# Hash attention with a squared-ReLU MLP: sign bits by eight small transfers in GpSimd's queue, weight exponents in four single steps, x in four pieces, the last pair's sums in another order

## Chip, cores and metric

The kernel runs on one core of a Trainium2 chip. The metric is device time in microseconds (us) of one execution; lower is better. The time before is a median of three runs. A profile of one execution shows every instruction of the engines TensorE (PE, with its weight loads as PEld), VectorE (DVE), ScalarE (ACT), GpSimd (POOL) and of SyncE (SP), which only issues transfers here.

## The reference, cut to what matters

```python
# q, k, v: (4, 8, 768, 64) float32; proj: (64, 6) float32
q_bits = (einsum('bhsd,dk->bhsk', q, proj) > 0)          # six sign bits of each query
k_bits = (einsum('bhsd,dk->bhsk', k, proj) > 0)          # and of each key
mask   = bucket(q_bits)[:, :, :, None] == bucket(k_bits)[:, :, None, :]
scores = where(mask, q @ k.T / 8, -1e9)
attn   = softmax(scores)                                 # sum + 1e-9 below the line
x      = (attn @ v) rearranged to (3072, 512)
out    = (max(x @ w_in, 0) ** 2) @ w_out                 # w_in (512, 2048), w_out (2048, 512)
```

`w_in` and `w_out` arrive as 64-bit floats, and the kernel makes 32-bit floats of them itself, from the two 32-bit halves of each number.

## The kernel before

**Two parts.** The first 334 us are the attention; the rest is the MLP, written as nested sums and differences of blocks (a Strassen-like scheme) and not touched by the change, apart from where its first inputs are prepared. Engine instructions run in the order in which the program issues them (`tc.manual_schedule()`), each engine in its own queue; waits between engines are put in by dependency.

**The attention loop** goes over 16 pairs of heads (`for pr in range(NP)`, pairs 0 to 15). Six key blocks of 128 keys (`kt`) and two halves of 384 queries (`i`) make twelve steps of `score` in a pair. A `score` multiplies first the bits (`st<-bits`, L431) and then the features (`st<-feat`, L431) into a PSUM buffer `st`; the bits add a large negative number wherever the buckets differ. ACT then writes `e`, the exponential (`weight`, L437). Two buffers of the ring `turn` serve `st` and the hash products; `e` has a ring of four. `attend` (L487) multiplies `e` with the values, in order written out by hand between the scores, and `add_up` (L469, L474, on DVE) sums `e` over key blocks into `total`. `sum_up` (L536) sums `total` over partitions into `tot`, `invert` (L549 to L559) and `spread` (L570) make reciprocals of it, and `normalize` (L579, L585) scales the pair's result and stores it in the DRAM buffer `x_all`. `sum_up`, `invert`, `spread` and `normalize` of a pair run inside the next pair.

**GpSimd's queue.** `attend` and `sum_up` change row halves of PE now and then; at each such point `part` (L482) puts a `memset` of a single element, `token`, in POOL's queue. It waits for the last matmul before the change, and the first one behind it waits for the token. There are four in a pair: at `attend(pr, 0, 1)`, `attend(pr, 2, 0)`, the old pair's `attend(old, 4, 1)`, and in `sum_up`. POOL does nothing else in the loop, except that at pair 12 (`X_0`) it issues the load of the MLP's first chunk of x, `load_x(0)` (L639), 2 MB in a single transfer.

**The bits of the next pair.** Early in a pair PE makes the products with `proj` (`hash_bits`, L365) for the next pair. ACT takes the sign (L384) and multiplies by per-partition gains (L387) into the SBUF tile `signed`, whose partitions are four groups (queries or keys, first or second half) of 32. ACT's own queue stores `signed` in DRAM (`bits_d`, L388). In `place_bits` (L395), behind `score(pr, 4, 0)`, ACT's queue loads it back with two transfers that put the rows where the score needs them, in `all_bits`, double-buffered over pairs.

**The weights.** In each pair one piece of a weight (128 x 1024 numbers) is turned: `part_power` (L151, DVE) cuts the exponent out, `place_power` on ACT converts it in two halves (`g`) of two operations each (L164 to `small`, L165 back to `power`), `part_top` (L173, L177, DVE) and `round_weight` (L191, L194, DVE) finish it. `sum_in` (L601, DVE) forms sums of the pieces of `w_in`, one or two in some pairs. SP issues the loads of the pieces, the loads of q, k (`load_pair`, L305) and v (L314), the stores of `x_all` (L590) and of the weights' sums (L219).

**The end of the attention.** Behind the loop DVE makes four differences of x (`sum_x(0, n)`, L601, tiles `t_x`) for the first MLP product, among the last pair's `add_up`, `invert` and `normalize`. PE begins the MLP (`acc`, L824) right after the last `spread`.

Of the kernel before, what the change touches and what calls it, by code (L numbers as in the profile page):

```python
# [8 lines left out]
FP32 = mybir.dt.float32  # L9
BF16 = mybir.dt.bfloat16  # L10
# [3 lines left out]
U8 = mybir.dt.uint8  # L14
ACTF = mybir.ActivationFunctionType
# [19 lines left out]
def kernel(  # L35
# [10 lines left out]
    nc = tc.nc  # L46
    PSUM = bass.MemoryType.PSUM

    B, H, S, D = q.shape
    NBITS = proj.shape[1]  # L50
    DM = H * D
    DFF = moe_w_in.shape[1]
    P = 128
    SB = S // P
    HS = S // 2
    NFT = DM // P
    NFF = DFF // P
    NP = B * H // 2
    PB = H // 2
# [49 lines left out]
    def spare(name):  # L109

        return ps_t.tile([P, 2, 512], FP32, name=name, tag="spare")
# [42 lines left out]
        )  # L154
        parts[i] = power

    def place_power(i, g):


        if i not in parts:  # L160
            return
        power = parts[i][:, g]
        small = p_w.tile([P, PIECE], U8, name="small", bufs=1)
        nc.scalar.activation(out=small, in_=power, func=ACTF.Relu, bias=excess)  # L164
        nc.scalar.activation(out=power, in_=small, func=ACTF.Copy, scale=2.0**23)  # L165

    def part_top(i):

# [14 lines left out]
    def round_weight(i):  # L183

        raw = raws.pop(i, None)
        if raw is None:
            return keep_weight(i)
        goals[i] = goal(i)
        power, top = parts.pop(i)
        one = top.bitcast(FP32)  # L190
        nc.vector.scalar_tensor_tensor(  # L191
            out=one, in0=raw[:, :, :, 0], scalar=2.0**-32, in1=top, op0=ALU.mult, op1=ALU.add,
        )
        nc.vector.scalar_tensor_tensor(  # L194
            out=goals[i], in0=one, scalar=2.0**-20, in1=power.bitcast(FP32),
            op0=ALU.mult, op1=ALU.mult,
        )
        keep_weight(i)
# [43 lines left out]
    ring = [const.tile([P, 2, 2, HS + 1], FP32, name=f"e{i}") for i in range(NRING)]  # L242
    signed = const.tile([P, 2, HS], BF16, name="signed")
    all_bits = [const.tile([P, 2, S], BF16, name=f"bits{i}") for i in range(2)]
    bits_d = p_d.tile([P, 2, HS], BF16, name="bits_d")

    def constants():
        N = NBITS
# [132 lines left out]
    def signs(pr):  # L381


        nc.scalar.activation(  # L384
            out=signed, in_=hashed[pr, 0][:, :, 0:HS], func=ACTF.Sign, scale=HUGE, bias=lifts
        )
        nc.scalar.activation(out=signed, in_=signed, func=ACTF.Copy, scale=gains)  # L387
        nc.scalar.dma_start(out=bits_d, in_=signed)  # L388

    def place_bits(pr):  # L390

        t = all_bits[pr % 2]
        src = bits_d.rearrange("(g r) h c -> h r g c", r=NR_B)
        for h in range(2):
            nc.scalar.dma_start(  # L395
                out=t[h * D:h * D + NBITS + 1].rearrange("r w (c n) -> r (w c) n", c=2),
                in_=src[h, 0:NBITS + 1],
            )
        for w in range(2):
            bits[pr, w] = t[:, w]  # L400

    def first_keys(c, banks):

# [37 lines left out]
    def score(pr, kt, i, st=None):  # L441

        own = [feat[pr][:, w] for w in range(2)]
        marks = [bits[pr, w] for w in range(2)]
        st = st or turn("st")
        products(st, i, kt, marks, True)
        products(st, i, kt, own, False)
        weight(pr, kt, i, st)
# [44 lines left out]
    def attend(pr, kt, s):  # L493


        if (kt, s) == (0, 0):
            outs[pr] = ps_o.tile([P, 2, 512], FP32, name="xo")
        for r in range(2):
            for h in range(2):
                done = value(  # L500
                    pr, kt, slice(r * HK, (r + 1) * HK), h, (r + s) % 2,
                    (kt, s) == (0, 0), (kt, s) == (SB - 1, 1),
                )
                if turned.get(pr, s) != s:
                    part(lasts[pr], done)
                turned[pr] = s
        lasts[pr] = done
# [58 lines left out]
    def spread(pr):  # L566

        both = onces.pop(pr)
        for h in range(2):
            nc.tensor.matmul(  # L570
                out=spares[pr][h * D:(h + 1) * D, 0, HS:HS + 2 * NB], lhsT=picks,
                rhs=both[:, h].rearrange("p c n -> p (c n)"), start=True, stop=True,
            )
# [59 lines left out]

    xs = {}

    def load_x(i):

        x = p_c.tile([P, NFT, NCH], FP32, name="x")
        nc.gpsimd.dma_start(out=x, in_=x_all[:, :, i * NCH:(i + 1) * NCH])  # L639
        xs[i] = x, [p_c.tile([P, 2, NCH // 2], FP32, name=f"t_x{n}") for n in range(3)]  # L640

    w_unit = {}

# [5 lines left out]
    def load_unit(n, pool=p_i):  # L649

        if n < NCHUNK * NR and n not in w_unit:
            r = order(n)
            w_unit[n] = pool.tile([P, 7, NFT // 2, P], FP32, name="w_unit", bufs=2 if pool is p_i else 1)
            m = 7 if n < NR else 5
            nc.sync.dma_start(out=w_unit[n][:, 0:m], in_=w_in_7[r, :, 0:m])

    def sum_x(i, n):

        x, (t1, t2, t3) = xs[i]
        lo, hi = slice(0, NCH // 2), slice(NCH // 2, NCH)  # L660
        b11, b12, b21, b22 = x[:, 0:2, lo], x[:, 0:2, hi], x[:, 2:4, lo], x[:, 2:4, hi]
        minus(*((t1, b12, b11), (t2, b22, t1), (t3, b22, b12), (b12, b21, t2))[n - 1])

    with tc.manual_schedule():
# [21 lines left out]
        for pr in range(NP):  # L686
            more, old = pr + 1 < NP, pr - 1

            def beside(kt, s):
                if pr > 0:  # L690
                    attend(old, kt, s)

            if pr + 2 < NP:
                load_pair(pr + 2)
            if pr == X_0:
                load_x(0)
            if more and pr > 0:
                features(pr + 1)
            if pr == 0:
                first_score()  # L700
                first_keys(1, spare("hash"))
            else:
                score(pr, 0, 0)
                attend(old, 4, 0)
                score(pr, 0, 1)
                attend(old, 5, 0)
                add_up(old, SB - 1)
                if pr == 1:
                    part_top(0)
                round_weight(old)  # L710
                if more:
                    load_weight(pr + 1)
                for m in sums.get(pr, ()):
                    sum_in(m)
            score(pr, 1, 0)
            beside(4, 1)
            score(pr, 1, 1)
            beside(5, 1)
            if pr == 0:
                features(1)  # L720
            else:
                keep_x(old)
                sum_up(old, 0)
                if more:
                    hash_bits(pr + 1, turn("hash"))
                    signs(pr + 1)
                else:
                    score(pr, 2, 0)
                sum_up(old, 1)
                invert(old)  # L730
            add_up(pr, 1)


            if pr == X_0 + 1:
                for n in range(2):
                    load_unit(n)
            part_power(pr)
            if pr == 0:
                attend(pr, 0, 0)
            if more:  # L740
                score(pr, 2, 0)
            if pr > 0:
                attend(pr, 0, 0)
            else:
                attend(pr, 1, 0)
            score(pr, 2, 1)
            if pr > 0:
                attend(pr, 1, 0)
                place_power(pr, 0)
            else:  # L750
                hash_bits(1, turn("hash"))
                signs(1)
            score(pr, 3, 0)
            if pr > 0:
                spread(old)
            attend(pr, 0, 1)
            score(pr, 3, 1)
            attend(pr, 1, 1)
            add_up(pr, 2)
            if pr > 0:  # L760
                normalize(old)
                place_power(pr, 1)
            add_up(pr, 3)
            if more:
                load_values(pr + 1)


            score(pr, 4, 0)
            if more:
                place_bits(pr + 1)  # L770
            attend(pr, 2, 1)
            score(pr, 4, 1)
            attend(pr, 3, 1)
            if pr > 0:
                part_top(pr)
            score(pr, 5, 0)
            if more:
                attend(pr, 2, 0)
            score(pr, 5, 1, spare("st") if not more else None)
            attend(pr, 3, 0)  # L780
            if pr == 0:
                for g in range(2):
                    place_power(0, g)
            add_up(pr, 4)
        pr = NP - 1
        attend(pr, 2, 0)
        attend_whole(pr, SB - 2)
        sum_x(0, 1)
        add_up(pr, SB - 1)
        for s in range(2):  # L790
            sum_up(pr, s, True)
        invert(pr)
        for n in (2, 3):
            sum_x(0, n)
        attend_whole(pr, SB - 1)
        keep_x(pr)
        spread(pr)
        normalize(pr)
        sum_x(0, 4)
        round_weight(pr)  # L800
        first.close()

# [793 lines left out]
```

## Time and profile before

| | |
|---|---|
| time, median of 3 runs | 882.53 us (880.44, 882.53, 882.84) |
| the profiled execution | 881.52 us, its span 879.7 us |
| mean granted TensorE clock | 0.995 |
| PE, DVE, ACT, POOL busy | 859.9, 751.6, 353.0, 123.8 us |
| first matmul of the MLP | 334.2 us after the span's start |

The span is the time from the first to the last instruction. Busy time of matmuls is modelled, since they are pipelined: a PE that is busy all the time may still be waiting a little between two matmuls. In a timeline row the brackets give the idle time of the engine before the row and what ended it; `ACTq` and `SPq` are the issues of transfers. In group rows the numbers behind the bar are busy us and mean ns of one instruction, then idle us before them. In the chain of waits a row that begins with DMA is a transfer that something waited for.

### The profile page before, as it was taken

What the parts mean: (1) busy time and instruction counts of PE and PEld (TensorE: products, weight loads), DVE (VectorE), ACT (ScalarE), POOL (GpSimd) and SP (SyncE); (2) the same over time, 40 slices, a digit from 0 to 9 for tenths busy, and PEclk for the clock granted to TensorE, in tenths of its full rate; (3) what the DMA queues carried; (4) which work ended last, traced back from release to release, by engine and by line L of the source; (5) the groups of instructions that cost most, each with busy time, mean ns of one, the idle gap of its engine ahead of it and who ended that gap; (6) DMA issues with size and microseconds to landing.
All of it is one profiled execution on the core that took longest, in us unless ns stands there. A gap on an engine that the chain in (4) does not pass through costs nothing.

```text
span 879.7 us, 16684 instructions
## 1 busy us (share of the span) xinstructions
PE 859.9 (98%) x6612; PEld 538.5 (61%) x6612; DVE 751.6 (85%) x1021; ACT 353.0 (40%) x584; POOL 123.8 (14%) x230
## 2 busy tenths in 40 slices
PE   8999999999989999999999999999999999999996
PEld 3555554455545544444688865556888755568885
DVE  5899999999988988888779978888889788888875
ACT  5777777777766762222211123332111233321110
POOL 1000000000000000564022121111000211110002
PEclk9999999999999999999999999999999999999998
DMA  9668998899899424989788775436857744355565
GB/s 202 144 155 156 243 166 179 200 242 192 192 270 250 148 72 158 337 269 291 278 301 275 215 166 172 165 115 229 287 145 190 169 159 156 128 168 151 161 166 113
DMA packets 225951, 170.97 MB, mean 194 GB/s; under 512 B 164514, under 2 KB 184170, under 8 KB 225866
## 3 DMA queue, kind: packets, MB, share of 16 engines
q1 hardware_dynamic: 187744, 87.19, 40.4%
q10 hardware_dynamic: 25594, 41.36, 15.4%
q0 software_dynamic: 12528, 41.30, 15.0%
q8 instruction: 53, 0.87, 0.4%
q14 instruction: 32, 0.26, 0.1%
HBM read 125.17 MB, written 44.63 MB: 193 GB/s over the span
## 4 chain that ended last, share of the span: by engine, by line
PE 88%; DMA 5%; DVE 3%; ACT 2%; SPq 1%; issue 1%; ACTq 0%; POOL 0%; DVEq 0%; POOLq 0%
PE acc L824 40%; PE acc L1043 16%; PE st L431 14%; PE xo L487 11%; PE acc L996 5%; DMA bits<-bits_d 2%; PE tot L536 1%; SPq L305 1%; DMA qk_nat<-in_k_dram 1%; PE hash L365 1%; DMA w_in<-s_in 1%; DMA bits_d<-signed 1%; DVE total L474 1%; ACT e L437 1%; DVE total L469 0%
## 5 line engine op out<-in xcount | busy, mean ns | idle before, releaser
L437 ACT ACTIVATE e<-st 128x768 f32<-128x768 f32 x192 | 151.6, 809 | 79.7 <-PE st L431 67.5
L431 PE MATMUL st<-feat 64*64 64x384 f32 x1536 | 163.2, 485 | 1.0 <-DVE feat L334 1.0
L487 PE MATMUL xo<-e,v_nat 64*64 64x385 f32 (+1 forms) x1520 | 164.0, 488 | 0.0
L824 PE MATMUL acc<-b,leaf 128*128 128x256 f32 x600 | 133.1, 379 | 0.0
L824 PEld LDWEIGHTS acc<-b,leaf 128*128 128x128 f32 x600 | 113.8, 190 | 16.3 <-issue 0.9
L474 DVE TENSOR_TENSOR total<-total,e 128x1536 f32<-128x1536 f32 x64 | 111.8, 1747 | 6.3 <-ACT e L437 6.2
L487 PEld LDWEIGHTS xo<-e,v_nat 64*64 64x64 f32 (+1 forms) x1520 | 62.4, 134 | 56.5 <-issue 38.0
L1043 PE MATMUL acc<-t_x,w_unit 128*128 128x512 f32 x192 | 90.2, 592 | 0.0
L431 PEld LDWEIGHTS st<-feat 64*64 64x64 f32 x1536 | 62.6, 133 | 27.0 <-issue 22.1
L431 PE MATMUL st<-bits 64*64 64x384 bf16 x768 | 70.9, 328 | 6.5 <-ACT e L437 3.9
L824 PE MATMUL acc<-t,leaf 128*128 128x256 f32 x336 | 76.2, 380 | 0.0
L824 PEld LDWEIGHTS acc<-t,leaf 128*128 128x128 f32 x336 | 63.6, 190 | 9.2 <-DVE t L601 0.5
L908 DVE SCALAR_TENSOR_TENSOR b<-h 128x512 f32<-128x512 f32 x96 | 65.7, 691 | 3.0
L431 PEld LDWEIGHTS <-bits 64*64 64x64 bf16 x768 | 30.3, 106 | 50.6 <-issue 38.7
L1043 PE MATMUL acc<-x,w_unit 128*128 128x512 f32 x128 | 60.1, 592 | 0.0
L482 POOL MEMSET token<- 1x1 f32 x62 | 17.0, 275 | 302.9 <-PE xo L487 251.4
L824 PE MATMUL acc<-x,w_unit 128*128 128x512 f32 x128 | 56.5, 593 | 0.0
L1043 PEld LDWEIGHTS acc<-t_x,w_unit 128*128 128x128 f32 x192 | 36.5, 190 | 28.9 <-issue 26.8
L824 PE MATMUL acc<-b_t,leaf 128*128 128x256 f32 x240 | 53.8, 379 | 0.0
L824 PEld LDWEIGHTS acc<-b_t,leaf 128*128 128x128 f32 x240 | 45.5, 190 | 6.2
L831 ACT COPY two<-acc 128x256 f32<-128x256 f32 (+1 forms) x29 | 12.5, 432 | 87.7 <-PE acc L824 72.2
L831 ACT COPY one<-acc 128x256 f32<-128x256 f32 (+1 forms) x29 | 12.5, 432 | 79.2 <-PE acc L824 55.4
(159 smaller groups left out, 1189.9 us busy)
## 6 DMA issues: line engine op xcount, KB each, us to landing
leaf<-w_out ACTq DMA_DIRECT2D x142, 256.0 KB
w_unit<-w_in SPq DMA_DIRECT2D x16, 640.0 KB
raw<-in_moe_w_in_dram SPq DMA_DIRECT2D x8, 1024.0 KB
raw<-in_moe_w_out_dram SPq DMA_DIRECT2D x8, 1024.0 KB
w_unit<-w_in SPq DMA_DIRECT2D x8, 896.0 KB
w_out<-sums POOLq DMA_DIRECT2D x16, 448.0 KB, 6.9
sum<-w_in SPq DMA_DIRECT2D x16, 448.0 KB
v_nat<-in_v_dram SPq DMA_DIRECT2D x16, 384.0 KB
```

What stands on the lines that cost most here:

```text
L305: nc.sync.dma_start(out=both[g * 32:(g + 1) * 32, w].rearrange("i (c d) -> i c d", d=32), in_=src[b, 2 * j + h].rearrange("(c i) (e d) -> ...
L365: nc.tensor.matmul(out=banks[g * NR_B:(g + 1) * NR_B, h, 0:HS], lhsT=projs[rows], rhs=feat[pr][rows, w, c * HS:(c + 1) * HS], start=True, ...
L431: nc.tensor.matmul(out=st[k * HK:(k + 1) * HK, h, 0:HS], lhsT=src[1][rows, key], rhs=src[0][rows, cut], start=first, stop=not first, skip_ ...
L437: nc.scalar.activation(out=key_of(pr, kt)[:, :, i, 0:HS], in_=st[:, :, 0:HS], func=ACTF.Exp, scale=scale)
L474: nc.vector.tensor_tensor(out=totals[pr], in0=totals[pr], in1=e, op=ALU.add)
L482: step = nc.gpsimd.memset(token, 0.0)
L487: return nc.tensor.matmul(out=outs[pr][h * D:(h + 1) * D, c, 0:HS + 1], lhsT=nat[pr, "v_nat"][rows, h, kt * D:(kt + 1) * D], rhs=key_of(pr ...
L824: nc.tensor.matmul(out=acc[to], lhsT=a(i), rhs=b(i), start=first and i == 0, stop=last and i == n - 1, skip_group_check=True,)
L831: nc.scalar.copy(out=t, in_=acc[of])
L908: nc.vector.scalar_tensor_tensor(out=out, in0=h, scalar=0.0, in1=h, op0=ALU.max, op1=ALU.mult)
L996: nc.tensor.matmul(out=out, lhsT=w[:, a], rhs=b, start=start, stop=stop, skip_group_check=True)
L1043: nc.tensor.matmul(out=acc[to], lhsT=w[:, PLACE[a], f], rhs=bt[b](f), start=first and f == 0, stop=last and f == NFT // 2 - 1, skip_group_ ...
```

## The change

- `signs` keeps only the sign; the multiplication by the gains becomes `weigh`, called later: before `score(pr, 3, 0)`, in pair 0 behind it. The DRAM buffer `bits_d` is gone.
- `place_bits` moves up to behind `attend(pr, 0, 1)` and issues eight transfers from `signed` to `all_bits` in POOL's queue, each of 7 partitions and 768 bytes a partition, first those that the next pair reads first.
- `place_power` does one of its two operations per call, and the four calls of a pair lie between different scores.
- `load_x(0)` becomes four transfers of 512 KB, at the end of pairs 9, 10, 11 and 12, behind `attend(pr, 2, 0)`. The first two `load_unit` go to pairs 13 and 14 instead of both to pair 13.
- In the last pair `part_top` moves behind the last `sum_x`, and `sum_x(0, 1)` behind `invert`.

```diff
-    def place_power(i, g):
+    smalls = {}
+
+    def place_power(i, g, s):
...
-        small = p_w.tile([P, PIECE], U8, name="small", bufs=1)
-        nc.scalar.activation(out=small, in_=power, func=ACTF.Relu, bias=excess)
-        nc.scalar.activation(out=power, in_=small, func=ACTF.Copy, scale=2.0**23)
+        if s == 0:
+            smalls[g] = p_w.tile([P, PIECE], U8, name="small", bufs=1)
+            nc.scalar.activation(out=smalls[g], in_=power, func=ACTF.Relu, bias=excess)
+        else:
+            nc.scalar.activation(out=power, in_=smalls[g], func=ACTF.Copy, scale=2.0**23)
...
+    def weigh():
+
         nc.scalar.activation(out=signed, in_=signed, func=ACTF.Copy, scale=gains)
-        nc.scalar.dma_start(out=bits_d, in_=signed)
 
     def place_bits(pr):
 
         t = all_bits[pr % 2]
-        src = bits_d.rearrange("(g r) h c -> h r g c", r=NR_B)
-        for h in range(2):
-            nc.scalar.dma_start(
-                out=t[h * D:h * D + NBITS + 1].rearrange("r w (c n) -> r (w c) n", c=2),
-                in_=src[h, 0:NBITS + 1],
-            )
-        for w in range(2):
+        for w, c in (1, 0), (0, 0), (0, 1), (1, 1):
             bits[pr, w] = t[:, w]
+            at = (2 * w + c) * NR_B
+            for h in range(2):
+                nc.gpsimd.dma_start(
+                    out=t[h * D:h * D + NBITS + 1, w, c * HS:(c + 1) * HS],
+                    in_=signed[at:at + NBITS + 1, h],
+                )
...
-    def load_x(i):
+    def load_x(i, fs=slice(0, NFT)):
-        x = p_c.tile([P, NFT, NCH], FP32, name="x")
-        nc.gpsimd.dma_start(out=x, in_=x_all[:, :, i * NCH:(i + 1) * NCH])
-        xs[i] = x, [p_c.tile([P, 2, NCH // 2], FP32, name=f"t_x{n}") for n in range(3)]
+        if i not in xs:
+            x = p_c.tile([P, NFT, NCH], FP32, name="x")
+            xs[i] = x, [p_c.tile([P, 2, NCH // 2], FP32, name=f"t_x{n}") for n in range(3)]
+        nc.gpsimd.dma_start(out=xs[i][0][:, fs], in_=x_all[:, fs, i * NCH:(i + 1) * NCH])
...
-            if pr == X_0:
-                load_x(0)
...
-            if pr == X_0 + 1:
-                for n in range(2):
-                    load_unit(n)
+            if pr in (X_0 + 1, X_0 + 2):
+                load_unit(pr - X_0 - 1)
...
                 attend(pr, 1, 0)
-                place_power(pr, 0)
+                if more:
+                    weigh()
+                else:
+                    place_power(pr, 0, 0)
...
             score(pr, 3, 0)
             if pr > 0:
                 spread(old)
+                place_power(pr, 0, int(not more))
+            else:
+                weigh()
             attend(pr, 0, 1)
+            if more:
+                place_bits(pr + 1)
...
                 normalize(old)
-                place_power(pr, 1)
+                if more:
+                    place_power(pr, 0, 1)
+                else:
+                    place_power(pr, 1, 0)
...
             score(pr, 4, 0)
             if more:
-                place_bits(pr + 1)
+                place_power(pr, int(pr > 0), 0)
+            else:
+                place_power(pr, 1, 1)
             attend(pr, 2, 1)
             score(pr, 4, 1)
+            if more:
+                place_power(pr, int(pr > 0), 1)
             attend(pr, 3, 1)
-            if pr > 0:
+            if 0 < pr < NP - 1:
                 part_top(pr)
             score(pr, 5, 0)
+            if pr == 0:
+                place_power(0, 1, 0)
             if more:
                 attend(pr, 2, 0)
+            if 2 * PB < pr <= 2 * PB + NFT:
+                load_x(0, slice(pr - 2 * PB - 1, pr - 2 * PB))
...
             attend(pr, 3, 0)
             if pr == 0:
-                for g in range(2):
-                    place_power(0, g)
+                place_power(0, 1, 1)
...
-        sum_x(0, 1)
         add_up(pr, SB - 1)
...
-        for n in (2, 3):
+        for n in (1, 2, 3):
             sum_x(0, n)
...
         sum_x(0, 4)
+        part_top(pr)
         round_weight(pr)
```

More of the change, by code (lines that the diff above doesn't have):

```diff
@@ L244 @@
     all_bits = [const.tile([P, 2, S], BF16, name=f"bits{i}") for i in range(2)]
-    bits_d = p_d.tile([P, 2, HS], BF16, name="bits_d")
     def constants():
```

## The prediction

> **What bounds the kernel now.** I read the page first, then the waits and the timeline of the first 335 us (the attention part, the only one edited), pair by pair.
>
> ```profile
> span 879.7 us, 16684 instructions
> PE 859.9 (98%) x6612; PEld 538.5 (61%) x6612; DVE 751.6 (85%) x1021; ACT 353.0 (40%) x584; POOL 123.8 (14%) x230
> ```
>
> PE is busy 98%. From 334.3 us (first `acc` matmul) to the end the chain of waits is PE without a break, so a microsecond won before 334.3 moves all the rest, and only PE's stalls before it can be won. The next view cuts the attention part at the first `tot` matmul of each pair (read off PE's timeline); columns are stretch, length, busy time of PE, PEld, DVE, ACT, POOL, then granted clock, DMA share, GB/s. By my count from `tot` of the old pair, the stretches are pairs 3, 4, 7, 9, 11, 12, 13, 14.
>
> ```profile
> 73.50:92.86 19.36, 19.36 (x297) 9.78 (x293) 17.88 (x18) 14.40 (x20) 1.21 (x4) 1.00 0.72 152
> 92.86:112.86 20.00, 19.69 (x297) 11.28 (x293) 19.22 (x20) 14.42 (x20) 1.20 (x4) 1.00 1.01 260
> 151.86:171.22 19.36, 19.36 (x296) 9.76 (x292) 18.48 (x19) 14.39 (x20) 1.22 (x4) 1.00 0.84 173
> 190.65:210.90 20.25, 19.70 (x296) 11.19 (x293) 19.98 (x21) 14.44 (x20) 1.23 (x4) 1.00 0.97 196
> 249.63:274.51 24.88, 21.56 (x297) 13.07 (x293) 20.32 (x21) 14.44 (x20) 0.87 (x4) 0.93 0.95 205
> 274.51:295.11 20.60, 19.92 (x295) 11.39 (x292) 18.49 (x18) 14.31 (x20) 1.20 (x4) 1.00 0.66 215
> ```
>
> An undisturbed pair takes 19.36 us. Pairs 4, 9, 12 and 13 exceed that by 0.64, 0.89, 5.52 and 1.24, together 8.29 us: the stock that can be won in the loop. In pairs 4, 9 and 13 (and 1.1 us of pair 12) the matmuls on `bits` wait for the DMA `bits<-bits_d`. Chain and timeline say why:
>
> ```profile
> 243.91 9.46 SPq L305 DMA_DIRECT2D qk_nat<-in_k_dram  x4
> ...
> 255.33 0.35 ACTq L388 DMA_DIRECT2D bits_d<-signed  x1
> 255.79 1.51 ACT L437 ACTIVATE e<-st 128x768 f32<-128x768 f32 x2 [2.97 <-DMA qk_nat<-in_k_dram]
> ...
> 241.79 0.91 POOL L639 DMA_DIRECT2D x<-x_all  x1 [0.29 <-issue]
> ...
> 277.73 7.09 DMA bits_d<-signed
> 284.89 3.90 DMA bits<-bits_d
> ```
>
> In pair 12 the 2 MB load of `x` (241.79) fills the DMAs; SP needs 9.46 us for four loads of 2 to 3 us, and ACT cannot issue `bits_d` until 255.33, though `signed` was ready at 252.8. The exps behind that issue come 2.5 us late, PE stands 2.9 us, and its granted clock then falls (0.79, 0.50 and 0.86 in the stretches 256:258, 258:260, 260:262). In pair 13 the store to DRAM takes 7.09 us and the load back 3.90, one after the other.
>
> **Bits by GpSimd.** Removed: per pair one ACT-issued store and two loads, with the round trip through DRAM. Added: eight transfers on POOL, issued between two of POOL's `token` memsets on which PE's `attend` waits.
>
> ```profile
> 156.58 0.62 POOL L482 MEMSET token<- 1x1 f32 x1 [3.88 <-PE xo L487]
> 162.67 0.42 POOL L482 MEMSET token<- 1x1 f32 x1 [5.47 <-PE xo L487]
> ...
> L861 POOL DMA_DIRECT2D raw_qk<-in_q_dram x32 | 17.3, 542 | 161.1 <-DVE peaks L865 160.9 <-DVE h L1030 0.2
> L1141 POOL DMA_DIRECT2D out_dram<-h x26 | 16.8, 655 | 173.5 <-DVE h L1134 169.5 <-DVE b_t L601 2.4 <-DVE most L886 1.5
> L1303 POOL DMA_DIRECT2D w_out<-sums x16 | 15.7, 985 | 13.1 <-DVE sums L595 11.0 <-DVE sums L597 2.0
> ```
>
> Worked in pair 7. `weigh` (0.935 us, row L387) comes after the exp of the second key block's second half: exps at 154.3 to 156.5, then `weigh` to about 157.4. POOL has its token done at 157.20, so the eight issues start at 157.5. No row shows an issue of 7 rows of 768 B. The nearest have 128 descriptors (L861: 0.54), 512 (L1141: 0.655), 896 (L1303: 0.985): cost falls with their number (a line through the first and the last gives 0.47 for seven), so I take the nearest row, 0.54, with 0.47 and 0.985 as the ends. Eight end at 157.5 + 4.3 = 161.8. The next token is due at 162.67 and is held by DVE's tensor_scalar L173 (162.37 to 163.06) to 163.09 anyway, so the issues are free up to 163.06, that is up to 0.695 each. In pair 0 no such hold exists: `weigh` ends near 21.5, issues at 25.8, token due at 25.20: 0.3 to 0.6 us lost there.
>
> Arrival: the next pair's first score reads at 165.0 what the first four carry, issued by 159.6; the idle row of raw_qk (issue to landing 2.6) gives 162, the loaded ones (5.9 to 6.9, four issues at 415.2 to 416.9) give 165 to 166. So the wait goes in most pairs; I leave 1 us for the five pairs whose DMAs are near 100% at that point (4, 8, 9, 12, 13). ACT issues no DMA in the loop any more, so 255.33 cannot recur.
>
> Moving `weigh` behind the exps brings them 1.4 us forward and removes PE's wait before the third key block (155.93 to 156.39, 0.16 over the usual 0.30). That gives nothing: the token of 156.58 is held to 157.20 by DVE's L151, and PE's next `attend` starts at 157.27, right behind it. I count 0, at most 0.16 x 14 = 2.2.
>
> **Weight exponents in four.** The same four ACT operations (0.72 and 0.63 twice), one between two exps instead of two. ACT is busy 14.4 of 19.36, so only lateness counts: the last now ends at about 163.4, and DVE's L177, which reads it, started at 162.97: 0.45 us of DVE. Cover: DVE idles 0.7 to 1.9 us in most pairs; in pair 9 it idles 0.27, but is late itself, so the wait shrinks. If the cover were gone it would be 0.45 a pair, 6 us. Pair 0 did all four together (28.07 to 30.86), and PE stood 1.24 at 30.37, 0.94 over normal: won. Net of the token, pair 0 gives 0.5.
>
> **x in four.** One 2 MB issue (0.91 us) becomes four of 512 KB behind POOL's second token in pairs 9 to 12; POOL is idle 5 us there, so the issues cost nothing. Each adds a quarter of the 9.6 us that the whole took to land, 2.4 us of DMA, to a pair; pairs 10 and 11 have that room, pair 9 (0.97) does not and hands on some 2 us. What SP loads there is read over 10 us later (`v_nat` issued at 161.24, read at 173.5). I take the whole 5.52 of pair 12 as won. `load_unit` one pair apart: 0.
>
> **The last pair.** First, ACT: the exp before 322.36 no longer waits for the 0.63 copy, so PE's 1.15 stall shrinks by 0.6. Second, DVE:
>
> ```profile
> 326.03 1.22 DVE L177 SCALAR_TENSOR_TENSOR power<-raw,power 128x1024 uint32<-128x1024 uint32 x1
> 327.16 1.75 DVE L474 TENSOR_TENSOR total<-total,e 128x1536 f32<-128x1536 f32 x1
> 328.83 1.22 DVE L601 TENSOR_TENSOR t_x<-x 128x1024 f32<-128x1024 f32 x1
> 329.97 1.75 DVE L474 TENSOR_TENSOR total<-total,e 128x1536 f32<-128x1536 f32 x1
> ...
> 331.77 0.86 PE L536 MATMUL tot<-total,ones 128*32 128x192 f32 x16 [1.92 <-DVE total L474]
> ```
>
> L173 + L177 (1.73) and the first `t_x` (1.14) leave the way to the last `total`: 2.9 less. But the two adds then wait for their exps, which I place at 326.2 (key block 4) and 327.8 (5): adds 326.2 to 327.95 and to 329.6, so `tot` at 329.65 instead of 331.77: 2.1 won, the 0.6 contained in it. Behind it DVE does t1, t2, t3 from 331.9 to 335.3; PE's product starts at 332.15 and reads t2 3.5 us later (334.2, in time). `round_weight` ends at 342.7, so the first gate is 0.9 later than before and 3 later against PE; accumulators are double over products of 12 us, so it costs nothing.
>
> **Sum.** 8.29 + 0.5 + 2.1 - 1.0 = 9.9 us. The profiled execution took 881.52 (span 879.7 and 1.8 around it), 1.0 under the median of 882.53: 881.5 - 9.9 = 871.6.
>
> **Rivals.** *POOL becomes the bound (slower).* Should a short SBUF-to-SBUF issue cost as much as L1303's 0.985, the eight end at 165.4, the second token is 2.3 us late, PE stands in each of 15 pairs: +35, about 906. It costs anything from 0.695 an issue and eats the whole gain of 9.9 (0.66 a pair) from (163.06 + 0.66 - 157.5) / 8 = 0.78. Against: issues of 128 descriptors follow each other every 0.53 to 0.58 (L861; L949 as well, at 452.23 and 452.78, though its durations read 0.85). For: no row has 7 partitions, and L1290 with 256 descriptors takes 0.735. 0.12.
>
> *Transfers one after another (slower).* If each waited for the one before to land, the fourth would land 4 x 2.6 = 10.4 after 157.5, at 167.9 instead of 165.0: 2.9 a pair, over 910. The trace speaks against: the four at 415.2 to 416.9 landed within 2.6 us of each other. 0.02. The Trainium skill, page "DMA: Bandwidth & Descriptors", section "Rules for kernel authors", says to merge many small transfers, since below 64 KB one pays mostly overhead, and its section on the anatomy of a DMA puts a fixed 2.0 us on each; by that in series the fourth would land at 165.5, an estimate. The overlapping landings are what this trace shows instead.
>
> *Bits still late.* In loaded pairs landing takes the 6.9 us of the row at 416.85: 1 us late in five pairs rather than 1 in all: 876. 0.15.
>
> *The x pieces move the stall.* Saturated pairs 9 to 11 hold SP back and half of pair 12's loss returns (2.8): 874.5. 0.10.
>
> *More than counted.* The token is not held and steady pairs win 0.16 each, bits are never late: 881.5 - 13.1 = 868.4. 0.18.
>
> *Nothing measurable*: issues of about 0.78, or late bits together with the moved stall. 0.05.
>
> **How the numbers follow.** My forecast has 0.38. Faster: 0.38 + 0.15 + 0.10 + 0.18 = 0.81. Same (within 0.3%, 2.6 us, about what a measurement can tell): 0.05. Slower: 0.14. The range runs from the upper case off the lowest run (880.4 - 13.1 = 867.3, rounded to 867) to the late bits with an issue at 0.735 as well (876 + 15 x 0.3 = 880.5, rounded to 881).
>
> **What would show it.** Right: pairs of 19.3 to 19.4 us throughout, clock 1.00 in pair 12; no wait for a DMA on `bits` over 0.5 us; POOL issues of 0.5 to 0.6 and `token` rows ending at the same place in the pair; `tot` of the last pair with a wait under 0.7. Wrong: PE's `xo` rows waiting for `token` by over 0.5 us in every pair, issues over 0.7, or DVE as what ends PE's waits.

## The result and the profile after

The changed kernel takes 871.98 us (median of four runs, 870.76 to 872.32), beside 882.63 (880.44 to 882.84) for the kernel before: a ratio of 0.9882, 95% interval 0.9864 to 0.9901. The forecast was 871.6. The profiled execution took 872.13 with a span of 870.3, where before it was 881.52 with 879.7: 9.4 us less. The head of the page:

```profile
span 870.3 us, 16839 instructions
PE 856.5 (98%) x6612; PEld 530.8 (61%) x6612; DVE 752.5 (86%) x1021; ACT 351.3 (40%) x584; POOL 185.3 (21%) x353
```

POOL's busy time rose by 61.5 us, which is 120 issues of 0.52 (in the trace, `bits<-signed` at L402, 520 ns mean). PE is still the engine of the chain. The view by stretches, cut at the first `tot` matmul as in the prediction, for pairs 3, 4, 7, 9, 12 and 13 (columns: stretch, length, busy time of PE, PEld, DVE, ACT, POOL, granted clock, DMA share, GB/s):

```profile
73.06:92.40 19.34, 19.34 (x296) 9.48 (x292) 17.96 (x18) 14.30 (x20) 5.30 (x12) 1.00 0.60 138
92.40:113.26 20.86, 19.82 (x297) 11.02 (x293) 19.93 (x20) 14.33 (x20) 5.30 (x12) 1.00 0.95 243
...
151.76:171.10 19.34, 19.34 (x296) 9.49 (x292) 18.64 (x19) 14.31 (x20) 5.30 (x12) 1.00 0.79 164
...
190.92:210.27 19.35, 19.35 (x296) 9.48 (x293) 18.71 (x20) 14.29 (x20) 5.89 (x13) 1.00 0.93 220
...
248.97:268.12 19.15, 19.15 (x297) 10.91 (x293) 18.95 (x20) 14.31 (x20) 4.99 (x13) 1.00 0.90 215
268.12:287.46 19.34, 19.34 (x296) 9.50 (x292) 18.64 (x19) 14.31 (x20) 5.29 (x12) 1.00 0.69 206
```

Pair 12 went from 24.88 to 19.15, pair 13 from 20.60 to 19.34, pair 9 from 20.25 to 19.35, and the clock of pair 12 from 0.93 to 1.00. Two things were not foreseen: pair 4 became longer (20.00 to 20.86), and pair 12 became shorter than an undisturbed pair. Where the 9.4 us came from, by stretches of the two traces:

| stretch | before, us | after, us | difference | forecast |
|---|---|---|---|---|
| start to pair 0's end | 34.64 | 34.27 | −0.37 | −0.5 |
| pairs 1 to 14 | 279.84 | 272.54 | −7.30 | −7.29 (8.29 less 1.0) |
| last pair, to the first `acc` | 19.76 | 17.27 | −2.49 | −2.1 |
| first `acc` to the end | 545.43 | 546.20 | +0.77 | 0 |

The timeline shows the mechanism in pair 4, in pair 7 (POOL and DVE) and in the last pair:

```profile
107.05 0.63 PE L436 MATMUL st<-bits 64*64 64x384 bf16 x4 [1.04 <-DMA bits<-signed]
...
156.48 0.61 POOL L487 MEMSET token<- 1x1 f32 x1 [3.88 <-PE xo L492]
157.73 4.08 POOL L402 DMA_DIRECT2D bits<-signed  x8 [0.65 <-ACT signed L393]
162.54 0.43 POOL L487 MEMSET token<- 1x1 f32 x1 [0.72 <-PE xo L492]
...
156.36 0.69 DVE L151 TENSOR_SCALAR power<-raw 128x1024 uint32<-128x1024 uint32 x1
...
162.25 0.69 DVE L177 TENSOR_SCALAR top<-raw 128x1024 uint32<-128x1024 uint32 x1
...
316.08 5.48 DVE L479 TENSOR_TENSOR total<-total,e 128x1536 f32<-128x1536 f32 x3
...
321.62 0.86 PE L541 MATMUL tot<-total,ones 128*32 128x192 f32 x16
```

The eight issues run from 157.73 to 161.81, nearly as placed, and POOL then idles 0.72 us before its next token. Both tokens end 0.03 to 0.04 us behind a tensor_scalar of DVE (157.09 after L151's end at 157.05, 162.97 after L177's at 162.94). In pair 4 the first `bits` land late. In the last pair the three adds (one row, 5.48 us) follow each other with 0.10 us between them, and `tot` has no wait.

### The profile page after: what moved, and what is told of

The parts are those of the page before. It is cut to its first block, busy times and chain, and to the rows that moved or that the text cites. A ratio compares the mean times of both kernels' runs of the same rounds, so it can differ in the third digit from the quotient of the medians.

```text
span 870.3 us, 16839 instructions
## 1 busy us (share of the span) xinstructions
PE 856.5 (98%) x6612; PEld 530.8 (61%) x6612; DVE 752.5 (86%) x1021; ACT 351.3 (40%) x584; POOL 185.3 (21%) x353
## 4 chain that ended last, share of the span: by engine, by line
PE 92%; DMA 3%; DVE 2%; POOL 1%; issue 1%; ACT 1%; POOLq 0%; DVEq 0%; ACTq 0%
PE acc L845 39%; PE acc L1064 16%; PE st L436 16%; PE xo L492 13%; PE acc L1017 6%; DMA bits<-signed 2%; PE tot L541 2%; PE hash L368 1%; DMA leaf<-w_out 1%; POOL bits L402 1%; DVE total L474 1%; ACT signed L393 0%; DVE flip L554 0%; DVE total L479 0%; ACT e L442 0%
## 5 line engine op out<-in xcount | busy, mean ns | idle before, releaser
L442 ACT ACTIVATE e<-st 128x768 f32<-128x768 f32 x192 | 155.8, 812 | 76.9 <-PE st L436 71.0
L492 PE MATMUL xo<-e,v_nat 64*64 64x385 f32 (+1 forms) x1520 | 161.4, 487 | 0.7 <-POOL token L487 0.6
L436 PE MATMUL st<-feat 64*64 64x384 f32 x1536 | 160.0, 483 | 1.0 <-DVE feat L337 1.0
L492 PEld LDWEIGHTS xo<-e,v_nat 64*64 64x64 f32 (+1 forms) x1520 | 58.6, 133 | 61.2 <-issue 43.8
L436 PEld LDWEIGHTS st<-feat 64*64 64x64 f32 x1536 | 59.9, 133 | 35.1 <-issue 31.0
L436 PE MATMUL st<-bits 64*64 64x384 bf16 x768 | 67.7, 325 | 1.4 <-DMA bits<-signed 1.2
L402 POOL DMA_DIRECT2D bits<-signed x120 | 61.5, 520 | 15.1 <-ACT signed L393 15.1
L1162 POOL DMA_DIRECT2D out_dram<-h x26 | 16.8, 654 | 173.9 <-DVE h L1155 166.8
L882 POOL DMA_DIRECT2D raw_qk<-in_q_dram x32 | 17.3, 541 | 162.9 <-DVE peaks L886 162.7
```

The source lines that it names most:

```text
L402: nc.gpsimd.dma_start(out=t[h * D:h * D + NBITS + 1, w, c * HS:(c + 1) * HS], in_=signed[at:at + NBITS + 1, h],)
L436: nc.tensor.matmul(out=st[k * HK:(k + 1) * HK, h, 0:HS], lhsT=src[1][rows, key], rhs=src[0][rows, cut], start=first, stop=not first, skip_ ...
L442: nc.scalar.activation(out=key_of(pr, kt)[:, :, i, 0:HS], in_=st[:, :, 0:HS], func=ACTF.Exp, scale=scale)
L492: return nc.tensor.matmul(out=outs[pr][h * D:(h + 1) * D, c, 0:HS + 1], lhsT=nat[pr, "v_nat"][rows, h, kt * D:(kt + 1) * D], rhs=key_of(pr ...
L882: nc.gpsimd.dma_start(out=raw_qk[i][:, w], in_=flat[:, i * n:(i + 1) * n])
L1162: queue.dma_start(out=out[at, m0 + a * 32:m0 + (a + 1) * 32].rearrange("(c i) j -> i c j", i=32), in_=ot[a * 32:(a + 1) * 32].rearrange("i ...
```

## Experiments

Letters and numbers of theories in the expectations are those of each run alone; e1, e5, e6 and e8 in them are the runs "x whole again", "The last pair's order undone", "Exponents in twos again" and "Tokens freed". "Pair" is a stretch as above, and a quiet pair is one that waits for no transfer.

**x whole again.** Does the gain of pair 12 need the four pieces?

```diff
+            if pr == X_0:
+                load_x(0)
...
-            if 2 * PB < pr <= 2 * PB + NFT:
-                load_x(0, slice(pr - 2 * PB - 1, pr - 2 * PB))
```

> The changed kernel with x loaded whole again, 2 MB at the start of pair 12. Theory A (pair 12 lost its 5.5 us because ACT had to issue a store while the DMAs were full; with no ACT issue in the loop the big load does no harm): at most 1 us slower than the changed kernel, about 872 to 873, pair 12 within 1 us of 19.35, from a late arrival of bits at most. Rival X (the 2 MB load itself is the cause, and only its split cures it): 4.4 to 5.5 us slower, 876 to 877.5, pair 12 near 24, granted clock below 1.00 there.

872.15 us (871.77 to 873.11), ratio 0.9881 (0.9853 to 0.9909): the same as with the pieces. Pair 12 by stretches:

```profile
247.01:267.36 20.35, 19.43 (x297) 11.76 (x293) 20.15 (x21) 14.31 (x20) 4.43 (x12) 1.00 0.93 206
```

The whole load still costs pair 12 about 1.0 us over 19.35 (its bits land late, and PE idles 0.92 us for them), but 4.5 of the 5.5 us are gone with the 2 MB in one piece, and the clock holds 1.00. ACT has no issue in its queue that could be held up. The remaining 1.0 is offset elsewhere (pair 4 took 19.34 in this execution).

**x in four, in the kernel before.** The counterpart: only the pieces, with the bits still in ACT's queue.

```diff
-            if pr == X_0:
-                load_x(0)
...
+            if 2 * PB < pr <= 2 * PB + NFT:
+                load_x(0, slice(pr - 2 * PB - 1, pr - 2 * PB))
```

> The kernel before with only x in four pieces (pairs 9 to 12). Theory A: the issue of the bits' store on ACT is still there, and pairs 9 to 12 have fuller DMAs, so a late store or late bits cost in some of them: 0 to 3 us faster than before, 880 to 882.5. Rival X: pair 12 falls to 20 us or below, 4.4 to 5.5 us faster, 877 to 878. Bits late in pairs 4, 9 and 13 by 0.6 to 1.2 us each in both.

880.13 us (877.73 to 887.03), ratio 0.9978 (0.9954 to 1.0002). Pairs 11, 12 and 13:

```profile
230.97:253.35 22.38, 20.09 (x296) 11.25 (x292) 20.06 (x21) 14.31 (x20) 1.73 (x5) 1.00 0.98 224
253.35:272.71 19.36, 19.36 (x296) 9.85 (x293) 17.52 (x17) 14.40 (x20) 1.72 (x5) 1.00 0.93 197
272.71:294.64 21.93, 19.95 (x296) 11.24 (x292) 19.54 (x20) 14.31 (x20) 1.21 (x4) 1.00 0.73 242
```

Pair 12 is cured, and its neighbours are ill: 22.38 and 21.93, with PE idle for 2.3 and 1.8 us at the bits, whose round trip through DRAM is now late there. Pair 9 went from 20.25 to 21.21 as well. The pieces alone move the loss. With the run before, this puts the loop's gain on the removal of ACT's issues and of the DRAM round trip; what each of these two is worth was not tried apart.

**Bits alone, in the kernel before.** Only the eight transfers and the moved `weigh`; exponents in pairs, x whole and the last pair as before.

```diff
-        nc.scalar.dma_start(out=bits_d, in_=signed)
...
+                nc.gpsimd.dma_start(
+                    out=t[h * D:h * D + NBITS + 1, w, c * HS:(c + 1) * HS],
+                    in_=signed[at:at + NBITS + 1, h],
+                )
```

> The kernel before with only the bits changed: sign and weigh apart, eight transfers in POOL's queue behind the first token; x whole at pair 12, exponents in two pairs of operations, last pair as before. Theory (this part carries the loop's gain; e1 and e6 put the others at about 0 and 1.4, e5 the last pair's order at about 2): 6 to 7.5 us faster than before, 875 to 876.5, pair 12 at or under 20.5. Rival (the loop's gain needs the parts together): 3 us or less faster, 879 or more.

876.81 us (875.84 to 877.78), ratio 0.9931 (0.9916 to 0.9947): some 6 of the 10.7 us, just short of the 6 to 7.5 that the theory gave.

```profile
249.38:269.63 20.25, 19.73 (x297) 11.14 (x293) 19.87 (x21) 14.22 (x20) 5.14 (x12) 1.00 0.94 214
```

Pair 12 takes 20.25, the other pairs 19.46 instead of 19.36, and the last pair's way to `tot` 17.29, as before. Pair 0 ends at 35.32 instead of 34.64: it pays for the token behind the eight issues, and has its four exponent steps still together.

**Exponents in twos again**, within the changed kernel:

```diff
                     weigh()
+                    place_power(pr, 0, 0)
+                    place_power(pr, 0, 1)
...
-                    place_power(pr, 0, 1)
+                    place_power(pr, 1, 0)
+                    place_power(pr, 1, 1)
```

> The changed kernel with the two exponent operations of a half together again, as in the kernel before (the first pair of them behind weigh and ahead of the third key block's exp; all four together in pair 0), the last pair left as changed. Theory 1 (only lateness counts and it is covered): pair 0 loses 0.9, the others nothing, about 872.9. Theory 2 (weigh and two exponent steps in a row hold up an exp by 2.3 us, PE waits 0.3 to 0.4 for an st buffer in each of 14 pairs): 5 to 6 us slower, 877 to 878.

873.35 us (873.07 to 873.73), ratio 0.9887 (0.9855 to 0.992), 1.4 over the changed kernel. Quiet pairs take 19.46 (0.11 more each) and pair 0 ends 1.15 later; pair 4, at 19.46, gives 1.4 of that back. So both theories hold a part: the pairing costs something in each pair, little, and most of what it costs at one place is in pair 0. The 19.46 is also what the bits alone showed: moving `weigh` behind the exps with paired exponents costs 0.1 a pair, and the four single steps take it back.

**The last pair's order undone**, within the changed kernel:

```diff
-            if 0 < pr < NP - 1:
+            if pr > 0:
                 part_top(pr)
...
+        sum_x(0, 1)
         add_up(pr, SB - 1)
...
-        for n in (1, 2, 3):
+        for n in (2, 3):
```

> The changed kernel with the last pair's DVE order of before (part_top inside the pair, the first sum_x ahead of the last add_up). Theory (these two lie on the way to the last total): the first MLP matmul comes 1.5 to 2.1 us later, 873.5 to 874.1. Rival (the gain at the end came from ACT's exponents alone): within 0.5 us of the changed kernel.

873.7 us (872.24 to 875.41), ratio 0.9887 (0.9854 to 0.992), 1.7 over the changed kernel. From its timeline:

```profile
322.92 0.86 PE L541 MATMUL tot<-total,ones 128*32 128x192 f32 x16 [2.53 <-DVE total L479]
...
326.17 4.50 PE L845 MATMUL acc<-x,w_unit 128*128 128x512 f32 x8
```

From the pair's start to `tot` it takes 17.29 us, exactly as in the kernel before, and 14.81 in the changed one: 2.48 us, and undoing the order on DVE loses all of it. So the exponents' finer steps on ACT, which this run keeps, win nothing here by themselves. Whether the new order alone would win the whole 2.48 was not tried: in the changed kernel the last add starts 0.09 us behind the end of its exp, and that exp ended 0.6 us later in the pair in the kernel before. PE idles 2.53 us, its granted clock reads 0.60 and 0.55 in the stretches 324:326 and 326:328, and the first eight `acc` matmuls take 4.50 us; in the changed kernel they take 3.70. After the 1.92 us of the kernel before the clock stayed at 1.00. So this execution, the slowest of the four, loses 1.6 us behind `tot` on top of the 2.48, and its loop is 1.6 us shorter (pair 4 took 19.41).

**Eight transfers in ACT's queue.** Does it matter whose queue?

```diff
-                nc.gpsimd.dma_start(
+                nc.scalar.dma_start(
```

> The changed kernel with the same eight transfers issued in ACT's queue instead of POOL's. If POOL as the issuer matters: eight issues of about 0.3 us (rows of before: 0.27 to 0.35) put 2.4 us between two exps, PE waits about 1 to 1.6 us for an st buffer in each of 14 pairs: 14 to 22 us slower than the changed kernel, 886 to 894, plus one more stall where the DMAs are full. If only the shorter path (no DRAM) matters: within 3 us of the changed kernel, 870 to 875.

961.15 us (960.5 to 963.14), ratio 1.0884 (1.0854 to 1.0914). ACT's timeline in a pair whose DMAs were nearly idle before the issues:

```profile
176.27 5.23 ACTq L402 DMA_DIRECT2D bits<-signed  x7
181.55 0.81 ACT L442 ACTIVATE e<-st 128x768 f32<-128x768 f32 x1 [4.75 <-DMA bits<-signed]
...
182.41 0.53 PE L436 MATMUL st<-bits 64*64 64x384 bf16 x4 [3.45 <-ACT e L442]
```

Seven issues take 5.23 us there, 0.75 each; nearly 5 us without an exp leave PE idle for 3.45 us, and the granted clock then reads 0.50 and 0.69 in the next two stretches of 2 us. An issue takes over twice the 0.27 to 0.35 that ACT's three issues took in the kernel before, and the loss is 89 us where 14 to 22 were expected. So the place of the issues decides: in POOL's queue the same eight cost nothing in a quiet pair, in ACT's they cost 5 us. SP's queue was not tried.

**Twelve transfers on POOL.** How many are free?

```diff
+            parts = 2 if (w, c) in ((0, 1), (1, 1)) else 1
+            n = HS // parts
...
+                for m in range(parts):
```

> The changed kernel with twelve transfers a pair, the last four of the eight halved in columns (same bytes). Theory (POOL's issues are free only until the second token is released, 163.06 in the example pair): issues of 0.52 end 157.73 + 6.24 = 163.97, the token is 0.9 us late in 14 pairs and about 2 in pair 0: 14 to 15 us slower, about 886. Rival (POOL's issues lie off the path altogether): within 1 us, 871 to 873.

901.83 us (899.74 to 903.78), ratio 1.0211 (1.0177 to 1.0246). Quiet pairs took 20.51 (1.16 more, where 0.9 was expected from the issues alone), pairs 4, 8 and 10 24.49, 23.65 and 24.13, and pair 0 5.0 us more, so the whole loss is twice the expected one. Pair 4 on POOL's and PE's timelines:

```profile
107.34 4.09 POOL L405 DMA_DIRECT2D bits<-signed  x8 [0.64 <-ACT signed L393]
114.10 2.05 POOL L405 DMA_DIRECT2D bits<-signed  x4 [2.67 <-DMA bits<-signed]
116.14 0.09 POOL L490 MEMSET token<- 1x1 f32 x1
...
116.28 1.56 PE L495 MATMUL xo<-e,v_nat 64*64 64x385 f32 x8 [3.47 <-POOL token L490]
```

The ninth issue waits 2.67 us until the first transfer has landed (at 113.82), and the token and PE wait behind it; the granted clock falls to 0.50 and 0.66 between 116 and 120. In the trace POOL's transfers signal eight semaphores in turn, and the ninth waits for the semaphore of the first. In quiet pairs the first has landed by then, and the twelve issues follow each other in 6.33 us. So in this program eight can be under way on POOL without waiting for a landing; the durations of the issues alone don't tell that.

**Four of the eight issued earlier**, ahead of the first token, with `weigh` straight behind `signs` and the other four left where they are:

```diff
                     signs(pr + 1)
+                    weigh()
...
-                    weigh()
+                    place_bits(pr + 1, ((1, 0), (0, 0)))
...
+                place_bits(pr + 1, ((0, 1), (1, 1)))
```

> The changed kernel with weigh right behind signs and the first four transfers issued ahead of the pair's first token, the other four behind it (pairs 1 to 14). Theory (pairs 4 and 8 lose 1.5 and 0.45 because the transfers land 7 us after their issue where the DMAs are full): both at 19.35, 1.9 us faster, about 870.1; the token is free at the same time, since four issues of 0.52 from 155.0 end at 157.1 where DVE holds it to 157.2 anyway. Rival: the four issues end behind the token's due time and cost 0.2 to 0.5 a pair: 3 to 7 us slower.

878.33 us (877.56 to 879.2), ratio 0.9949 (0.993 to 0.9968). The late bits are gone (pairs 4 and 8 take 19.95 and 19.94), but nearly every pair is that long (pairs 6, 9 and 12 take 19.64):

```profile
157.21 2.43 POOL L402 DMA_DIRECT2D bits<-signed  x4 [2.64 <-ACT signed L393]
159.63 0.09 POOL L487 MEMSET token<- 1x1 f32 x1
...
158.34 0.69 DVE L151 TENSOR_SCALAR power<-raw 128x1024 uint32<-128x1024 uint32 x1
```

This pair starts at 153.74, 2.0 us later than the one that the theory was worked in. The issues begin 0.2 us later in the pair than it said, and the third of the four takes 0.90 us instead of 0.52: it runs beside DVE's L151 and ends 0.09 us behind it. So the token ends at 159.72, 0.6 us behind the place where L151 would have let it go, and PE idles 0.59 us for it. The run's rival came true. It is the prediction's slower rival at another place: issues ahead of a token that nothing covers.

**Tokens freed.** The steady pair's 0.2 us. DVE's two tensor_scalars (L151, L177; the second is moved into `part_power`) are put ahead of the pair's own first add in pairs 1 to 14, away from the tokens:

```diff
                 invert(old)
+            if 0 < pr < NP - 1:
+                part_power(pr)
             add_up(pr, 1)
```

> The changed kernel with both tensor_scalars of the weights (exponent and mantissa) moved ahead of the pair's first add_up on DVE, so that neither runs while POOL has to write a token. Theory (steady pairs of 19.35 are held by the token, which waits for a DVE tensor_scalar; pairs 6 and 12, where DVE is late, already take 19.14): all pairs at 19.14, 11 x 0.21 = 2.3 us faster, about 869.7; the token rows at 0.09 instead of 0.61. Rival (something else sets 19.35): no change, 872, or slower because the adds come later.

869.29 us (867.99 to 871.0), ratio 0.9841 (0.9815 to 0.9867), a median 2.7 us under that of the changed kernel. The two were run beside different sets of the kernel before, and the intervals of their ratios just touch (0.9867 here, 0.9864 there). POOL's timeline in pair 7:

```profile
154.97 0.09 POOL L489 MEMSET token<- 1x1 f32 x1 [3.88 <-PE xo L494]
156.22 4.08 POOL L404 DMA_DIRECT2D bits<-signed  x8 [1.16 <-ACT signed L395]
160.91 0.09 POOL L489 MEMSET token<- 1x1 f32 x1 [0.60 <-PE xo L494]
```

Both tokens take 0.09 us instead of 0.61 and 0.43 (none of the kernel's 62 takes more than 0.09), and all quiet pairs take 19.14, as pairs 6 and 12 did already. Nine pairs went from 19.35 to 19.14, 1.9 us, and pair 1 won 0.3. Less late bits in pairs 4 and 8 give another 1.5, which differs between executions; 0.6 is lost in the last pair, where the moved tensor_scalar now stands ahead of the adds, and 0.7 before the loop and in the MLP. That makes the 2.3 us between the two spans; the theory's 2.3 is met by more than its own cause. The Trainium skill, page "SBUF — State Buffer", section "Who interferes with whom", says that VectorE and GpSimd share a pair of SBUF ports which a tensor_scalar can take for the whole instruction, so that the other "fully blocks"; the tokens of the changed kernel that end 0.03 to 0.04 us behind L177 and L151 agree with it, and so does this run.

**`weigh` one exp earlier**, on top of the freed tokens:

```diff
+            if more and pr > 0:
+                weigh()
             score(pr, 2, 1)
             if pr > 0:
                 attend(pr, 1, 0)
-                if more:
-                    weigh()
-                else:
+                if not more:
                     place_power(pr, 0, 0)
```

> e8 (tensor_scalars out of the tokens' way) with weigh one exp earlier, between the two exps of the third step's halves, so that the eight issues start about 0.8 us earlier behind a token that is now free. Theory: quiet pairs stay at 19.14, the late bits of pair 4 shrink by 0.8: 0 to 0.9 us faster than e8, 868.4 to 869.3. Rival (the exp behind weigh is now late for the st ring): 0.1 to 0.3 a pair, 1 to 4 us slower than e8.

869.73 us (869.22 to 870.28), ratio 0.985 (0.9833 to 0.9868). Pair 4 took 19.48 and pair 8 19.19, near the 19.14 of a quiet pair, but the first bits of pair 1 came 0.8 us late behind pair 0, and the total is that of the run before. How late the bits of pair 4 are differs between executions of nearly the same loop (0 to 1.5 us over the quiet pair: 20.86 in the changed kernel, 20.04 with freed tokens, 19.34 with x whole), so how much of this is owed to the edit stays open.

## Why the prediction was right

**Eight issues on POOL: right.** Each takes 0.52 us (0.54 was taken, from the row with the fewest descriptors), the eight end at 161.81 (161.8), below the 163.06 that DVE's L173 was to cover. That the end agrees to 0.01 is luck: the issues start 0.2 us later than placed, and eight of them are 0.2 us shorter. Neither the rival of POOL as the bound nor that of transfers in series took place: the issues follow each other every 0.52, and the landings overlap. The twelve transfers show how near the first of them was, and a limit that neither names: the ninth issue waits for the first landing.

**Bits late: mis-sized, and offset by chance.** The step left 1.0 us over five pairs. The trace has 1.5 in pair 4 and 0.5 in pair 8, together 2.0, because landing takes 1.5 us with idle DMAs but up to 7.8 with full ones (median 4.0; 6.3 to 7.8 in pair 4). Two of the signs that were to show it right fail here: PE waits 1.04 us for the bits in pair 4 (0.5 was the limit), and pairs 4 and 8 leave the 19.3 to 19.4 us. What kept the loop's sum at −7.30 beside −7.29 is 1.0 us of gains that the sum did not have. The stock was 8.8 us rather than 8.29, since pairs 1, 6 and 8 also stood over 19.36 before, pair 6 at 19.64. And in pairs 6 and 12 DVE runs late, so that its tensor_scalars start with the token or just behind it (137.38 against 137.33 in pair 6); the token then takes 0.09 us, and these pairs take 19.14, 0.21 less than a quiet one. The rest is hundredths over the other pairs. So the agreement to 0.01 is luck.

**The token holds ACT's gain back: right.** The prediction gave 0 for the exps that come 1.4 us earlier, since the token is held to L151's end, with 2.2 as its upper case. Quiet pairs went from 19.36 to 19.35. The freed tokens show the other side: with L151 and L177 moved, a quiet pair takes 0.21 us less.

**x in four: right in size for pair 12, wrong in its reason.** The 5.52 were counted as won by the pieces. x whole gives the same time (with pair 12 at 20.35, 4.5 of the 5.5 us won without the pieces); the pieces alone, in the kernel before, give a ratio of 0.9978 with 1 in its interval. So two things cure pair 12, each without the other, and only one of them wins the time: that the bits no longer go through ACT's queue and DRAM, which alone brings pair 12 to 20.25. The prediction names it too ("255.33 cannot recur") but prices it at nothing of its own.

**Weight exponents: the 0 was right beside the kernel before, not by itself.** Quiet pairs are as long as before, but the runs with paired exponents have 19.46: moving `weigh` costs 0.1, the single steps take it back. Pair 0's gain of 0.5 measured 0.37; PE waits 0.59 us there at 26.15 for the token that stands behind the eight issues (0.3 to 0.6 was given).

**The last pair: right in kind, 0.4 too small.** The term that was mis-sized is the wait of two adds for their exps, placed at 326.2 and 327.8, or 11.7 and 13.3 us after the pair's start. In the trace the exps end 11.0 and 12.9 us after it, and each add starts about 0.1 us behind its exp, with 0.10 us of idle time; so `tot` comes 2.48 us earlier instead of 2.1. The run with the order undone loses the same 2.48. It shows that ACT's part wins nothing alone, not that it is nothing: the adds of the new order start right behind the exps.

**The tail: missed by 0.77.** The step said that a microsecond won before the first `acc` moves all the rest. Of the 10.2 won there, 0.77 was given back. Half (0.39) lies at 436.25, where PE waits for a `leaf` that takes 8.53 us from issue to landing. Its load is issued 103.5 us after the first `acc` in both traces, so PE is not early for it; why it lands too late stays open. The runs above whose first `acc` comes by 330 us lose 0.3 to 1.4 us in this part of the MLP, those where it comes at 333 us or later at most 0.15. The other 0.4 lie at the end of the kernel; their cause was not tried.

**The sum of the parts.** By medians, the bits alone give about 6 us, the last pair's order 1.7 (2.48 in the trace up to `tot`), the exponents 1.4, the split of x 0.2. Together 9.3 of 10.7; with intervals of 1 to 3 us on each, the rest is not told apart from noise or interplay.

## What to carry to other kernels

Where a transfer is issued counts, and so does how many are under way: look in the trace for an engine that has idle time between two of its own dependants, add up the issues at the rate of the nearest row, and compare with the time at which its next instruction is due. An issue in the queue of an engine that feeds the bottleneck costs nothing while the engine has time to spare (ACT's three in a quiet pair of the kernel before: 19.36 us with them, 19.35 without), but eight of them cost 5 us a pair, and one that was held up by full DMAs most of 5.5 us in pair 12. And when a faster producer gains nothing, look at what else ends at the same moment: here a 0.09 us memset stretched to 0.6 beside another engine's instruction hid 0.2 us in most pairs.

## What the runs showed of the hardware

- The issue of the same small transfer (7 partitions of 768 B, SBUF to SBUF) took 0.52 us in POOL's queue and 0.71 to 0.75 in ACT's, where the DRAM store of before took 0.35. The Trainium skill, page "DMA: Bandwidth & Descriptors", section "SWDGE vs HWDGE vs iDMA", calls the path of ACT's queue "faster setup but less flexible" than GpSimd's; for the time that the issuing engine is held, the runs here show the opposite.
- A ninth POOL transfer waits for the landing of the first where that is late (2.67 us in pair 4 of the run with twelve).
- Landing of such a transfer ranges from 1.5 us to 7.8 with the load of the DMAs.
- Beside a tensor_scalar of DVE (0.69 us) POOL's memset of one element took up to 0.64 us instead of 0.09, and one of its issues 0.90 instead of 0.52; both ended less than 0.1 us behind the tensor_scalar. A memset that started 0.05 us ahead of it took 0.09.
- Behind idle times of PE of 3.45 and 3.47 us the granted clock reads 0.50 to 0.69 for about 4 us, so that they cost more than themselves (in the pair of the twelve with 3.47 us of idle time PE is also busy for 21.02 us, where it is for 19.34 in a quiet pair of the changed kernel). Behind 2.53 us it reads 0.60 and 0.55 from 1.1 us on, behind 1.92 it stayed at 1.00.
